# Chunked attention and a bilinear FFN on one core: reordering the first two attention units, and placing the third one step earlier

## The chip, the cores and the metric

The kernel runs on one core of a Trainium2 chip. The metric is the device time of one execution in microseconds (us); lower is better. A run counts as slow when it takes over 1.5% more than the fastest run of its kernel. In the profile lines PE is TensorE, PEld its weight loads, ACT ScalarE, DVE VectorE, POOL GpSimd, SPq the queue of transfers; the granted clock is the share of TensorE's full clock that the profile records. The profile's "span" is shorter than the device time by about 1.8 us, so spans are compared with spans and times with times.

## The reference, cut to what matters

```python
def _attn_ref(q, k, v):                 # B = H = 8, S = 576, D = 64
    q_c = q.reshape(B, H, nc, chunk, D) # chunks of 64 rows attend only to themselves
    scores = scale * np.matmul(q_c, k_c.transpose(0, 1, 2, 4, 3))
    attn = np.exp(scores - np.max(scores, axis=-1, keepdims=True))
    attn = attn / (np.sum(attn, axis=-1, keepdims=True) + 1e-09)
    return np.matmul(attn, v_c).reshape(B, H, S, D)

def _moe_ref(x, w_a, w_b, w_out):       # x: 4608 x 512, d_ff = 1536
    return (x @ w_a) * (x @ w_b) @ w_out
```

The attention output, transposed to tokens x 512, is the `x` of the second function.

## The kernel before: the parts that matter

The 4608 tokens are 18 *units* of 256 for attention and 9 *blocks* of 512 for the FFN. In the traces TensorE's matmuls come in the order in which the program is written (in the timeline below: scores at 13.59, block 0 at 19.65, transposes at 36.14 us), so the schedule is the order of calls. For one unit:

- `cast`: GpSimd (VectorE for q and k of unit 0) turns the loaded float32 q, k and v into bf16 (`q_raw`, `k_raw`, `v_raw`). The weight slices are cast there too, in one queue.
- `transpose_pe`: TensorE transposes q and k; VectorE and ScalarE copy the result to `qkt`.
- `scores`: 32 small matmuls into PSUM, then exp on ScalarE into `E`.
- `sums`: four matmuls with ones, then on ScalarE `ln` and `rs = exp(-ln)`, the inverse of the row sums.
- `values`: 32 small matmuls `E` x v, then VectorE multiplies by `rs` into `xT`, the FFN's input.

`ab_step(K, ft)` is one of the twelve FFN steps of block K, counted from 0: eight matmuls of 512 columns (`wb` and `wa`, four each), a ScalarE copy and a VectorE multiplication. Block 0 needs units 0 and 1. Block 1 begins with the half of it that is unit 2.

```python
        scores(0)                 # prologue, before block 0
        transpose_pe(1)
        sums(0)                   # units 0 to 2: ln, rs, ln, rs, by halves
        scores(1)
        values(0)
        sums(1)
        values(1)
        load(2, "qk")             # after five of the six weight slice pairs
        load_ab(5)
        load(2, "v")
        ...                       # (cut) casts in the same order
        for ft in range(NFT):     # block 0, NFT = 12
            ab_step(0, ft)
            if ft == 7:
                transpose_pe(2)
            if ft == 8:
                slot(2)           # scores(2)
            if ft == 10:
                slot(None, 2)     # sums(2), values(2)
```

The softmax here doesn't subtract the row's maximum and nothing guards it: scores larger than these inputs give would overflow.

## Time and profile before

| What | Value | Where it is read |
|---|---|---|
| time | 330.01 us median of the first three runs (329.94 to 330.35); the profiled run took 330.88 us | list of runs |
| span of the profiled run | 329.1 us | head of the page |
| first block-0 matmul | 19.65 us | timeline |
| k of unit 2 cast | 33.08 to 34.12 us | timeline |
| first block-1 matmul | 45.99 us, after 1.11 us idle | timeline |
| span left after that | 329.1 - 45.99 = 283.1 us | worked out |

The page's chain that ended last, kernel before (share of the span by engine):

```profile
PE 93%; ACT 3%; DMA 1%; DVE 1%; issue 0%; SPq 0%
```

TensorE is the limit. The waits of TensorE in the kernel before (who waited for whom: us in total, times, longest):

```profile
PE ps L156 <- DVE q_raw L144: 5.4, 1, 5.4
PE ps L278 <- DVE xT L239: 3.8, 2, 2.7
PE ps L186 <- ACT qkt L164: 1.6, 2, 1.4
...
```

The first line is the wait for the first q at the start, which the change leaves alone. The second is the two waits that the change is aimed at: 2.7 us before block 0 and 1.1 us before block 1, both for `xT`. The third, and others like it in the prologue, are waits for copies and exp. After 60 us no wait is longer than 0.2 us. Lines of the timeline of the kernel before, picked from all engines (start us, us, engine, line, operation, tiles, and in brackets the idle time before it and what ended it):

```profile
13.59 0.64 PE L186 MATMUL ps<-qkt 64*64 64x64 bf16 x32 [1.23 <-DVE qkt L164]
14.20 0.63 ACT L216 ACTIVATE rs<-ln 128x512 f32<-128x512 f32 x1
14.73 1.07 ACT L194 ACTIVATE E<-ps 128x512 bf16<-128x512 f32 x2
16.47 0.60 ACT L212 ACTIVATE ln<-ps 128x512 f32<-128x512 f32 x1 [0.67 <-PE ps L201]
19.65 1.87 PE L278 MATMUL ps<-xT,wb_162 128*128 128x512 bf16 x4 [2.74 <-DVE xT L239]
33.08 1.04 POOL L144 CAST k_raw<-k_in 128x1024 bf16<-128x1024 f32 x1 [0.97 <-DMA k_in<-in_k_dram]
36.14 0.61 PE L156 MATMUL ps<-identity,k_raw 128*128 128x128 bf16 x8
45.99 0.60 PE L278 MATMUL ps<-xT,wb_162 128*128 128x256 bf16 x4 [1.11 <-DVE xT L239]
```

Two things are to be seen. The scores of unit 1 are done at 14.23 us (13.59 + 0.64), but their exp starts at 14.73 us, as ScalarE ends the inverses of unit 0 (14.83 us; the records overlap a little). The Trainium skill, "TensorE: Matmul & The Clock Gate", Part 1 (Architectural detail), calls ScalarE's queue strict FIFO; this agrees. And k of unit 2 arrives late: its cast ends at 34.12 us, two microseconds before its transposes at 36.14 us.

The four matmuls from 19.65 us take 1.66 us (the next four start at 21.31 us), where four take 0.86 us later on. The same page says in Part 1 that the array starts at half clock. The trace agrees, with 0.43 against 0.216 us for a matmul.

### The profile page before, as it was taken

The page shows a single profiled execution, that of the slowest core. Times are in us where ns is not written, and L with a number is a line of the kernel's source. Part 1 is how long each engine was busy: PE and PEld are TensorE (multiplying, and loading weights), DVE is VectorE, ACT ScalarE, POOL GpSimd, SP SyncE. Part 2 cuts the span into 40 slices and gives each one's busy share as a digit, 9 for nine tenths or more (in the row PEclk, how much of TensorE's full clock was granted, in tenths as well). Part 3 has the DMA queues.
Part 4 walks back from the last instruction along what each step waited for, and adds up shares of the span by engine and source line. Part 5 has one row for each costly group of instructions (what it writes and reads, how often), then busy time and mean ns, then how long its engine had stood idle before and what let it go on. Part 6 is the DMA issues. An engine that isn't in the chain of part 4 may idle for free.

```text
span 329.1 us, 6671 instructions
## 1 busy us (share of the span) xinstructions
PE 311.4 (95%) x2712; PEld 157.4 (48%) x2712; DVE 133.9 (41%) x209; ACT 126.7 (38%) x224; POOL 73.7 (22%) x76
## 2 busy tenths in 40 slices
PE   2669989999999999999999999999999999999994
PEld 1424558776444444444444444444444444444441
DVE  3423454554443434343434343444344434433331
ACT  1633567257352525252525252525252524212200
POOL 1575556632222232132232211200000000000000
PEclk9999999999999999999999999999999999999999
DMA  8999899998979998999988918911120112012114
GB/s 241 320 383 293 225 371 257 276 214 197 173 198 248 228 224 192 225 210 253 203 207 211 231 34 147 241 31 34 42 54 3 34 34 64 1 32 63 35 32 96
DMA packets 139166, 53.91 MB, mean 164 GB/s; under 512 B 114560, under 2 KB 132992, under 8 KB 139136
## 3 DMA queue, kind: packets, MB, share of 16 engines
q1 hardware_dynamic: 139136, 53.49, 68.2%
q8 instruction: 21, 0.34, 0.4%
q14 instruction: 9, 0.07, 0.1%
HBM read 37.75 MB, written 9.44 MB: 143 GB/s over the span
## 4 chain that ended last, share of the span: by engine, by line
PE 93%; ACT 3%; DMA 1%; DVE 1%; issue 0%; SPq 0%
PE ps L278 57%; PE ps L294 28%; PE ps L201 2%; PE ps L156 2%; PE ps L186 2%; PE ps L230 1%; DMA k_in<-in_k_dram 1%; ACT rs L216 1%; ACT ln L212 1%; ACT qkt L164 1%; DVE xT L239 0%; DVE k_raw L144 0%; DVE o_sb L302 0%; ACT E L194 0%; SPq L129 0%
## 5 line engine op out<-in xcount | busy, mean ns | idle before, releaser
L286 ACT CAST b_sb<-ps 128x512 bf16<-128x512 f32 (+1 forms) x120 | 64.4, 546 | 142.6 <-PE ps L278 141.4
L287 DVE TENSOR_TENSOR ab_sb<-ps,b_sb 128x512 bf16<-128x512 f32 (+1 forms) x120 | 75.6, 637 | 94.1 <-PE ps L278 89.7
L294 PEld LDWEIGHTS <-ab_sb 128*128 128x128 bf16 x432 | 42.3, 98 | 50.1
L302 DVE COPY o_sb<-ps 128x512 f32<-128x512 f32 x36 | 24.9, 692 | 56.8 <-PE ps L294 56.8
L239 DVE TENSOR_TENSOR xT<-ps,rs 128x512 bf16<-128x512 f32 x36 | 23.4, 687 | 32.3 <-ACT rs L218 27.6
L144 POOL CAST q_raw<-q_in 128x1024 bf16<-128x1024 f32 x17 | 17.7, 1042 | 60.3 <-DMA q_in<-in_q_dram 52.0
L212 ACT ACTIVATE ln<-ps 128x512 f32<-128x512 f32 x36 | 19.9, 596 | 26.4 <-PE ps L201 26.4
L144 POOL CAST k_raw<-k_in 128x1024 bf16<-128x1024 f32 x17 | 17.7, 1042 | 47.9 <-DMA k_in<-in_k_dram 47.7
L278 PE MATMUL ps<-xT,wb_162 128*128 128x512 bf16 (+1 forms) x80 | 20.2, 378 | 3.8 <-DVE xT L239 3.8
L144 POOL CAST v_raw<-v_in 128x1024 bf16<-128x1024 f32 x18 | 18.8, 1042 | 17.7 <-DMA v_in<-in_v_dram 13.3
L294 PE MATMUL ps<-wo_437,ab_sb 128*128 128x512 bf16 x72 | 21.4, 379 | 0.0
L294 PE MATMUL ps<-wo_443,ab_sb 128*128 128x512 bf16 x72 | 21.4, 379 | 0.0
L294 PE MATMUL ps<-wo_433,ab_sb 128*128 128x512 bf16 x72 | 21.4, 379 | 0.0
L294 PE MATMUL ps<-wo_439,ab_sb 128*128 128x512 bf16 x72 | 21.4, 379 | 0.0
L294 PE MATMUL ps<-wo_441,ab_sb 128*128 128x512 bf16 x72 | 21.4, 379 | 0.0
L294 PE MATMUL ps<-wo_435,ab_sb 128*128 128x512 bf16 x72 | 21.4, 379 | 0.0
L194 ACT ACTIVATE E<-ps 128x512 bf16<-128x512 f32 x36 | 19.3, 587 | 1.8 <-PE ps L186 1.8
L278 PE MATMUL ps<-xT,wa_164 128*128 128x512 bf16 (+1 forms) x80 | 19.7, 370 | 0.0
L278 PE MATMUL ps<-xT,wb_186 128*128 128x512 bf16 (+1 forms) x80 | 18.9, 359 | 0.0
L278 PE MATMUL ps<-xT,wb_170 128*128 128x512 bf16 (+1 forms) x80 | 18.9, 359 | 0.0
L278 PE MATMUL ps<-xT,wb_182 128*128 128x512 bf16 (+1 forms) x80 | 18.8, 358 | 0.0
L278 PE MATMUL ps<-xT,wb_409 128*128 128x512 bf16 (+1 forms) x80 | 18.8, 358 | 0.0
(60 smaller groups left out, 324.5 us busy)
## 6 DMA issues: line engine op xcount, KB each, us to landing
out_dram<-o_sb SPq DMA_DIRECT2D x72, 128.0 KB, 2.4
v_in<-in_v_dram SPq DMA_DIRECT2D x32, 256.0 KB, 4.2
q_in<-in_q_dram SPq DMA_DIRECT2D x23, 256.0 KB, 3.9
k_in<-in_k_dram SPq DMA_DIRECT2D x23, 256.0 KB, 3.7
wst<-in_moe_w_b_dram SPq DMA_DIRECT2D x6, 512.0 KB, 7.3
wst<-in_moe_w_a_dram SPq DMA_DIRECT2D x6, 512.0 KB, 8.0
wst<-in_moe_w_out_dram SPq DMA_DIRECT2D x6, 512.0 KB, 7.2
q_in<-in_q_dram SPq DMA_DIRECT2D x4, 512.0 KB, 5.3
```

Source lines behind the costliest of these rows:

```text
L144: eng.tensor_copy(out=raw[n, U], in_=staged.pop((n, U)))
L156: nc.tensor.transpose(tp[:, i, m, :], src[:, i, 2 * m:2 * m + 2, :].rearrange("p j d -> p (j d)"), identity,)
L186: nc.tensor.matmul(sc[j][cl * 64:cl * 64 + 64, m, g, :], t[j * 64:j * 64 + 64, 1, g, m, cl * 64:cl * 64 + 64], t[j * 64:j * 64 + 64, 0, g, ...
L194: nc.scalar.activation(out=E_of[U][:, j], in_=sc[j], func=AF.Exp, scale=scale)
L201: nc.tensor.matmul(sm[cl][j * 64:j * 64 + 64, :], ones[cl * 64:cl * 64 + 64, :], E[cl * 64:cl * 64 + 64, j].rearrange("p m g s -> p (m g s)"),
L212: nc.scalar.activation(out=ln[:, cl].rearrange("p m n -> p (m n)"), in_=sm[cl], func=AF.Ln)
L239: nc.vector.tensor_tensor(out=x_tiles[K][:, :, c0:c0 + 128], in0=av[cl].rearrange("p m g s -> p m (g s)"), in1=rs[:, cl], op=MULT,)
L278: nc.tensor.matmul(ps[n], w_ab[n, i][:, kt, o:o + 128], xT[:, kt, c0:c1], start=(kt == 0), stop=(kt == NKT - 1),)
L286: nc.scalar.copy(out=b_sb[:, :c1 - c0], in_=ps["wb"])
L287: nc.vector.tensor_tensor(out=ab_tiles[K][:, ft, c0:c1], in0=ps["wa"], in1=b_sb[:, :c1 - c0], op=MULT)
L294: nc.tensor.matmul(o_ps, ab_tiles[K][:, ft, tg * 128:tg * 128 + 128], w_out[ft], start=(ft == 0), stop=(ft == NFT - 1),)
L302: nc.vector.tensor_copy(out=o_sb, in_=o_ps)
```

## The change

Its intent is to shorten both idle stretches. In the prologue, q of unit 1 is transposed before the scores of unit 0, in time in which TensorE waits, and ScalarE computes exp of unit 1 before the inverses of unit 0, which are now one instruction. In block 0, all three parts of unit 2's attention come one step earlier (transposes after step 6, scores after 7, sums and values after 9), and its inverse is one instruction as well.

```diff
-    def transpose_pe(U):
+    def transpose_pe(U, names="qk"):      # q and k can be transposed in two calls
...
-    def sums(U):
+    def sums(U, halves=False):            # None: leaves the inverse to the caller
...
+    def inverse(U, cl=None):              # rs = exp(-ln): one half, or both at once
...
+        transpose_pe(1, "q")
         scores(0)
-        transpose_pe(1)
-        sums(0)
+        transpose_pe(1, "k")
+        sums(0, halves=None)
         scores(1)
+        inverse(0)
         values(0)
-        sums(1)
+        sums(1, halves=True)
         values(1)
...
             ab_step(0, ft)
+            if ft == 6:
+                transpose_pe(2)
             if ft == 7:
-                transpose_pe(2)
-            if ft == 8:
                 slot(2)
-            if ft == 10:
+            if ft == 9:
                 slot(None, 2)
```

More of the change, by code (lines that the diff above doesn't have):

```diff
@@ L147 @@
     qkt = {}
-    def transpose_pe(U):
-        qkt[U] = qkt_pool.tile([128, 2, 2, NKT, 128], BF16, name="qkt")
-        for w, n in ((0, "q"), (1, "k")):
+    def transpose_pe(U, names="qk"):
+        if U not in qkt:
+            qkt[U] = qkt_pool.tile([128, 2, 2, NKT, 128], BF16, name="qkt")
+        for n in names:
+            w = "qk".index(n)
             src = raw.pop((n, U))
@@ L175 @@
     E_of = {}
+    ln_of = {}
     rs_of = {}
@@ L207, in sums @@
                 )
-        ln = sm_pool.tile([128, 2, NKT, 128], FP32, name="ln")
+        ln_of[U] = sm_pool.tile([128, 2, NKT, 128], FP32, name="ln")
         rs_of[U] = sm_pool.tile([128, 2, NKT, 128], FP32, name="rs")
@@ L212, in sums @@
             nc.scalar.activation(
-                out=ln[:, cl].rearrange("p m n -> p (m n)"), in_=sm[cl], func=AF.Ln
+                out=ln_of[U][:, cl].rearrange("p m n -> p (m n)"), in_=sm[cl], func=AF.Ln
             )
-            if U < 3:
-                nc.scalar.activation(out=rs_of[U][:, cl], in_=ln[:, cl], func=AF.Exp, scale=-1.0)
-        if U >= 3:
-            nc.scalar.activation(out=rs_of[U], in_=ln, func=AF.Exp, scale=-1.0)
+            if halves:
+                inverse(U, cl)
+        if halves is False:
+            inverse(U)
+    def inverse(U, cl=None):
+        for c in [slice(0, 2)] if cl is None else [cl]:
+            nc.scalar.activation(
+                out=rs_of[U][:, c], in_=ln_of[U][:, c], func=AF.Exp, scale=-1.0
+            )
     def values(U):
```

## The prediction

> **What bounds the kernel now.** TensorE. The chain of waits puts 93% of the 329.1 us span on it, and the table of waits shows no TensorE wait above 0.2 us after 60 us. So the change can only win what TensorE waits for before block 1, whose first matmul starts at 45.99 us. The timeline shows there: (a) 0 to 19.65 us, the prologue, ending in 2.7 us idle for xT of unit 1; (b) 19.65 to about 24.2 us, 512-column matmuls 0.43 us apart, 0.216 us afterwards. The Trainium skill, "TensorE: Matmul & The Clock Gate", Part 1, says that the array starts at half clock until about 3.4 us of sustained work in a free-running window; this trace agrees (4.6 us slow), though the page's clock row shows full clock; (c) 1.11 us idle at 45.99 us for xT of unit 2.
>
> **Prologue, costed.** q of unit 1 is cast at 8.74 us, so its transposes run while TensorE now idles (7.9 to 9.3 us). Their issue (0.83 us) pushes the scores of unit 0 back about 0.3 us. Both k copies on VectorE then start at about 11.25 instead of 12.25 us, scores of unit 1 at about 12.6 instead of 13.59. Moving exp of unit 1 (1.09 us) ahead of the inverse (1.06 us, measured on the 128x1024 form) keeps it early: sums of unit 1 at about 14.45 instead of 15.85 us, then 0.3 us lost behind the inverse. Last xT near 17.8, first block-0 matmul near 18.5 instead of 19.65: 1.1 us earlier, of which between half and all survives the slow clock, which may be released at the same moment as before.
>
> **Why that is mostly lost.** Attention of unit 2 needs k_raw(2), whose cast on GpSimd ends at 34.12 us behind a DMA wait; casts and loads there wait only for DMA and each other (DMA share 1.11 in this stretch), so they do not move. With transposes after step 6, TensorE would be there at about 33.3 to 33.8 us. I expect a new wait of 0.3 to 0.9 us of the k transposes for k_raw(2), and they start near 34.16 whatever the prologue won. Today's equivalent is 36.14 less one step (1.73), 34.41: net 0.25 us.
>
> **Why the second part pays.** Two steps (3.46 us) then cover the chain ln, ln, inverse, two xT. With one 1.06 us inverse that chain needs about 4.0 us from the sums; values and two steps give 4.1 us. The 1.11 us idle falls to about 0.1. From 34.16: transposes 0.44, five steps 8.65, scores 0.38, sums and values 0.64, waits 0.1: block 1 starts at about 44.4 instead of 45.99 us. v_raw(2) (39.89) and wa of step 10 (38.08) are just in time.
>
> **After.** The later inputs have slack (transposed k of unit 6 lands near 77 us for scores at 80), so about 1.6 us is carried to the end. Matmul count is unchanged.
>
> **Predicted: 328.4 us**, 80% range 327.7 to 329.4. Faster by over 2%: 0.01; within 2%: 0.98; slower: 0.01.
>
> **What would show it.** First block-0 matmul at 18.3 to 18.8 us; a new TensorE (or weight load) wait for k_raw(2), the cast still ending near 34.1 us; idle before block 1 below 0.4 us; start of block 1 at 44.2 to 44.8; then a constant shift of all stages.
>
> **What would make it wrong.** The clock is released a whole window (3.4 us) earlier or later; TensorE then waits longer, or not at all, for k_raw(2), but block 1 hardly moves unless release is late. The loads of unit 2 arrive at another time. The single inverse keeps xT of unit 2 late (up to 0.5 us). A later transposed load turns out to have no slack, so that part of the gain returns as a wait.

## The result, and the profile after

Six runs of each kernel: before 330.22 us median (329.94 to 331.31), after 329.30 us median (329.01 to 329.49). The ratio is 0.9963, with a 95% interval of 0.9946 to 0.9981. Ratios here are the mean time of one kernel's fast runs over that of the other's in the same rounds, so they are not quite the ratio of the medians quoted. The span of the profiled run fell from 329.1 to 327.5 us.

TensorE's waits in the changed kernel (same columns as above; L287 was L278, L158 was L156):

```profile
PE ps L287 <- DVE xT L248: 2.9, 1, 2.9
...
PE ps L158 <- POOL k_raw L144: 0.6, 1, 0.6
...
```

The wait for `xT` now occurs once; the one before block 1 is gone. A wait for `k_raw` has appeared. The same lines of the changed kernel's timeline:

```profile
12.87 0.64 PE L189 MATMUL ps<-qkt 64*64 64x64 bf16 x32 [0.62 <-DVE qkt L166]
13.55 1.09 ACT L197 ACTIVATE E<-ps 128x512 bf16<-128x512 f32 x2 [0.23 <-PE ps L189]
14.52 1.06 ACT L225 ACTIVATE rs<-ln 128x1024 f32<-128x1024 f32 x1
15.46 0.60 ACT L214 ACTIVATE ln<-ps 128x512 f32<-128x512 f32 x1
18.65 1.86 PE L287 MATMUL ps<-xT,wb_162 128*128 128x512 bf16 x4 [2.90 <-DVE xT L248]
32.86 1.04 POOL L144 CAST k_raw<-k_in 128x1024 bf16<-128x1024 f32 x1 [1.12 <-DMA k_in<-in_k_dram]
33.96 0.62 PE L158 MATMUL ps<-identity,k_raw 128*128 128x128 bf16 x8 [0.56 <-POOL k_raw L144]
44.28 0.60 PE L287 MATMUL ps<-xT,wb_162 128*128 128x256 bf16 x4
```

Exp of unit 1 starts at 13.55 instead of 14.73 us, and block 0 at 18.65 instead of 19.65 us. The transposes of k of unit 2 start 0.06 us after the end of its cast (32.86 + 1.04 = 33.90 us). Block 1 starts at 44.28 instead of 45.99 us, 1.71 us earlier, without idle time. From there the span takes 327.5 - 44.28 = 283.2 us, against 283.1 us before (282.9 us in a second profile of it, f4). The small loss is in one place: the scores of unit 6 start 0.53 us after their slot's sums (0.24 us before), and the wait is seen on the weight loads (window 76 to 80 us):

```profile
PEld L189 <- DMA qkt<-k_raw: 0.4, 1, 0.4
```

### The profile page after: what moved, and what is told of

Read it like the earlier page. It is cut to its first block, busy times and chain, and to the rows that moved or that the text cites. A ratio compares the mean times of both kernels' runs of the same rounds, so it can differ in the third digit from the quotient of the medians.

```text
span 327.5 us, 6667 instructions
## 1 busy us (share of the span) xinstructions
PE 311.7 (95%) x2712; PEld 157.3 (48%) x2712; DVE 133.8 (41%) x209; ACT 126.0 (38%) x222; POOL 73.5 (22%) x76
## 4 chain that ended last, share of the span: by engine, by line
PE 80%; DMA 7%; SPq 7%; DVE 1%; ACT 1%; POOL 1%; issue 1%; POOLq 0%; DVEq 0%
PE ps L287 49%; PE ps L303 26%; SPq L117 4%; DMA q_in<-in_q_dram 3%; SPq L129 3%; DMA v_in<-in_v_dram 3%; PE ps L189 1%; DMA qkt<-k_raw 1%; PE ps L239 1%; PE ps L204 1%; DVE qkt L166 1%; ACT rs L225 1%; POOL v_raw L144 1%; POOL q_raw L144 1%; PE ps L158 1%
## 5 line engine op out<-in xcount | busy, mean ns | idle before, releaser
L144 POOL CAST k_raw<-k_in 128x1024 bf16<-128x1024 f32 x17 | 17.7, 1040 | 44.7 <-DMA k_in<-in_k_dram 42.5
L144 POOL CAST v_raw<-v_in 128x1024 bf16<-128x1024 f32 x18 | 18.7, 1040 | 18.9 <-DMA v_in<-in_v_dram 16.2
L287 PE MATMUL ps<-xT,wb_162 128*128 128x512 bf16 (+1 forms) x80 | 20.1, 375 | 2.9 <-DVE xT L248 2.9
L287 PE MATMUL ps<-xT,wa_164 128*128 128x512 bf16 (+1 forms) x80 | 19.7, 370 | 0.0
L225 ACT ACTIVATE rs<-ln 128x1024 f32<-128x1024 f32 (+1 forms) x19 | 19.2, 1012 | 0.6
L287 PE MATMUL ps<-xT,wb_186 128*128 128x512 bf16 (+1 forms) x80 | 18.9, 359 | 0.0
L287 PE MATMUL ps<-xT,wb_170 128*128 128x512 bf16 (+1 forms) x80 | 18.9, 359 | 0.0
L287 PE MATMUL ps<-xT,wb_182 128*128 128x512 bf16 (+1 forms) x80 | 18.8, 358 | 0.0
```

The lines of the kernel that those rows point to most:

```text
L144: eng.tensor_copy(out=raw[n, U], in_=staged.pop((n, U)))
L225: nc.scalar.activation(out=rs_of[U][:, c], in_=ln_of[U][:, c], func=AF.Exp, scale=-1.0)
L287: nc.tensor.matmul(ps[n], w_ab[n, i][:, kt, o:o + 128], xT[:, kt, c0:c1], start=(kt == 0), stop=(kt == NKT - 1),)
```

## The experiments

Theory A: each part of the change would save about a microsecond, but both together are stopped by the arrival of unit 2's k, so they do not add up; later, the transposed load of unit 6 is the next such stop. Rivals: the parts add up (B); the prologue's gain is lost to the slow clock (C); the loads are no limit and the clock is (F, G, H in the texts below). Every run gave a correct result. The first two runs and g1, g2 cut the change into parts, the others move or remove one suspected limit.

### f1: the prologue alone

The changed kernel, with the places of unit 2 set back.

```diff
-            if ft == 6:
+            if ft == 7:
                 transpose_pe(2)
-            if ft == 7:
+            if ft == 8:
                 slot(2)
-            if ft == 9:
+            if ft == 10:
                 slot(None, 2)      # in slot: sums(f, halves=f == 2), two half inverses
```

> The new order of the prologue alone; attention of unit 2 stays at step 7 with its two half inverses. Theory A (the change's two parts overlap: each is bounded by the load of k of unit 2): first block-0 matmul at about 18.65 us, as with both; the k transposes of unit 2 come only at about 35 us, after its cast (34 us), so no wait for k_raw; the 1.1 us idle before block 1 stays; block 1 starts about 1.0 to 1.2 us before that of the kernel before (44.8 to 45.0 us); time -0.9 to -1.2 us. Rival B (parts add up): this part alone is worth the total, 1.6 us in the profiles, less the 1.1 us idle, so about 0.5 us. Rival C (the prologue gain is lost to the slow clock): block 1 moves by less than 0.6 us.

Measured: 330.05 us median (329.35 to 330.61) against 331.02 us of before in the same rounds, ratio 0.9976 (0.9961 to 0.9991). TensorE timeline of f1:

```profile
18.35 1.86 PE L287 MATMUL ps<-xT,wb 128*128 128x512 bf16 x4 [3.29 <-DVE xT L248]
34.72 0.62 PE L158 MATMUL ps<-identity,k_raw 128*128 128x128 bf16 x8
44.58 0.60 PE L287 MATMUL ps<-xT,wb 128*128 128x256 bf16 x4 [1.10 <-DVE xT L248]
```

The first block-0 matmul was 0.3 us earlier than expected (this run had an early clock release in the prologue, see i1). The cast of k ended at 34.66 us, so its transposes were held up by 0.1 us at most (they start 0.54 us after those of q at 34.18 us, where 0.45 us is usual), and the 1.1 us idle stayed. Block 1 started 1.4 us earlier than before. About 0.5 us of that is this run's clock (0.3 us at the start of block 0, and 5.47 instead of 5.68 us from its first step to its third); the 0.9 us left are still more than the 0.6 us that rival C allows, so in the trace it falls.

### f2: the steps alone

The changed kernel with the old prologue (calls joined on one line):

```diff
-        transpose_pe(1, "q"); scores(0); transpose_pe(1, "k"); sums(0, halves=None)
-        scores(1); inverse(0); values(0); sums(1, halves=True); values(1)
+        scores(0); transpose_pe(1); sums(0, halves=True)
+        scores(1); values(0); sums(1, halves=True); values(1)
```

> Attention of unit 2 one step earlier with one inverse, prologue as before. Theory A: first block-0 matmul at 19.65 us; the k transposes reach their place at about 34.4 us, just after the cast of k_raw(2) (34.1 us), so no or little wait (below 0.3 us); idle before block 1 falls from 1.1 to below 0.2 us; block 1 starts at about 44.5 to 44.8 us; time -1.1 to -1.4 us. With f1 the two sum to 2.0 to 2.6 us, more than both together give (1.6 us): the difference, 0.5 to 0.8 us, is the wait for k_raw(2) that only both together show. Rival B (additive): f1 and f2 sum to what both give, and no wait for k_raw(2) differs.

Measured: 329.90 us median (329.33 to 330.19), ratio 0.9966 (0.9952 to 0.9979). TensorE timeline of f2:

```profile
19.63 1.87 PE L287 MATMUL ps<-xT,wb 128*128 128x512 bf16 x4 [2.74 <-DVE xT L248]
34.92 0.61 PE L158 MATMUL ps<-identity,k_raw 128*128 128x128 bf16 x8
45.23 0.60 PE L287 MATMUL ps<-xT,wb 128*128 128x256 bf16 x4
```

There is no wait for k and no idle time before block 1. Block 1 was later than expected (45.23, not 44.5 to 44.8 us) because the clock came late in this run: the third step began 6.2 us after the first, against 5.7 us before and 5.5 us in the changed kernel. Without that, from the third step to block 1 (the former at 25.33, 25.84 and 24.16 us): before 20.66 us, f2 19.39 us, both parts together 20.12 us. The steps save 1.27 us alone but only 0.54 us with the new prologue. The missing 0.73 us is the wait for `k_raw` of the changed kernel, which shows as 0.7 us on its weight loads.

In the times, f1 and f2 save 0.24% and 0.34%, 0.58% or 1.9 us together; both in one kernel save 0.37%, or 1.2 us. The intervals are too wide for the times alone to decide this; the traces decide it.

### g1 and g2: the two halves of the prologue

Both have the old places for unit 2, so that k of unit 2 does not interfere. g1 keeps only the earlier transposes of q, g2 only the earlier exp (each against f1):

```diff
 # g1
-        sums(0, halves=None); scores(1); inverse(0); values(0)
+        sums(0, halves=True); scores(1); values(0)
 # g2
-        transpose_pe(1, "q"); scores(0); transpose_pe(1, "k")
+        scores(0); transpose_pe(1)
```

> Half of the prologue's change: q of unit 1 transposed ahead of the scores of unit 0, but exp of unit 1 still behind both half inverses of unit 0 (attention of unit 2 as before). Theory A (the two halves only pay together, since what one lets go is then held by the other): scores of unit 1 come about 0.7 us earlier (near 12.9 us) but exp of unit 1 starts at about 14.5 us, 0.2 us earlier than before, because the four ln and inverse passes hold ScalarE until then. First block-0 matmul at 19.4 to 19.6 us; time -0.1 to -0.3 us, within noise of the kernel before. Rival D (moving q is what pays): first block-0 matmul near 18.7 us, time -0.8 us.

> The other half: exp of unit 1 ahead of one inverse of unit 0, q of unit 1 transposed where it was. Theory A: scores of unit 1 at 13.6 us as before, exp of unit 1 at about 14.3 us instead of 14.73, and then ln of unit 1 waits for the inverse until about 16.3 us instead of 16.47: first block-0 matmul at 19.4 to 19.6 us; time -0.1 to -0.3 us. g1 and g2 together then give less than half of the 1.0 us that both show in one kernel. Rival E (the order of ScalarE is what pays): near 18.7 us, time -0.8 us.

Measured: g1 330.07 us median, ratio 0.9987 (0.9970 to 1.0005); g2 330.10 us, ratio 0.9988 (0.9970 to 1.0007). The timelines of g1 and then of g2, exp of unit 1, ln of unit 1 and the first block-0 matmul:

```profile
14.53 1.06 ACT L197 ACTIVATE E<-ps 128x512 bf16<-128x512 f32 x2
16.27 0.60 ACT L214 ACTIVATE ln<-ps 128x512 f32<-128x512 f32 x1 [0.67 <-PE ps L204]
19.45 0.58 PE L287 MATMUL ps<-xT,wb 128*128 128x512 bf16 x1 [2.74 <-DVE xT L248]
```

```profile
14.29 1.08 ACT L197 ACTIVATE E<-ps 128x512 bf16<-128x512 f32 x2 [0.76 <-PE ps L189]
15.26 1.06 ACT L225 ACTIVATE rs<-ln 128x1024 f32<-128x1024 f32 x1
16.21 0.60 ACT L214 ACTIVATE ln<-ps 128x512 f32<-128x512 f32 x1
19.39 0.58 PE L287 MATMUL ps<-xT,wb 128*128 128x512 bf16 x1 [2.90 <-DVE xT L248]
```

Each half wins 0.20 to 0.26 us at the start of block 0; together they win 1.00 us. In g1 the scores came at 12.85 us, but exp waited for the four passes of unit 0 until 14.53 us. In g2 exp was early, but ln of unit 1 then waited behind the inverse until 16.21 us. What one half frees, the part that was not changed takes back. Rivals D and E fall. Block 1 did not start earlier than before in either profile (46.22 and 46.12 us).

### f3: one step earlier still

```diff
-            if ft == 6:
+            if ft == 5:
                 transpose_pe(2)
-            if ft == 7:
+            if ft == 6:
                 slot(2)
-            if ft == 9:
+            if ft == 8:
                 slot(None, 2)
```

> The changed kernel with attention of unit 2 one step earlier still (after steps 5, 6 and 8). Theory A: the k transposes would be due at about 31.7 us but wait for the cast of k_raw(2) at 33.9 us: a wait of about 2.2 us instead of 0.6; v_raw(2) (cast ends 40.1 us) is then waited for too, by about 1.6 us less what has been lost already, since its values come one step (1.73 us) earlier; block 1 starts near 46 us, time about 1.3 to 1.8 us over the changed kernel, so about as the kernel before. A rival, that an earlier attention simply helps or does nothing: equal to the changed kernel or faster.

Measured: 331.86 us median (330.62 to 335.57), ratio 1.0050 (1.0006 to 1.0093). The profiled run is the slowest of the six (1.50% above the fastest). Its TensorE timeline:

```profile
34.35 0.62 PE L158 MATMUL ps<-identity,q_raw 128*128 128x128 bf16 x8 [3.76 <-POOL q_raw L144]
36.04 1.04 PE L158 MATMUL ps<-identity,k_raw 128*128 128x128 bf16 x8 [1.07 <-POOL k_raw L144]
36.87 1.91 PE L287 MATMUL ps<-xT,wb 128*128 128x512 bf16 x4
```

The inputs of unit 2 came two microseconds later than in the profile of the changed kernel (k's cast ended at 35.98 instead of 33.90 us), and the wait did more harm than its length: the matmuls after it take 1.71 us for four. The stretches of this run (from:to, length, busy time of each engine, granted clock, DMA share, GB/s):

```profile
34.00:35.00 1.00, 0.62 (x8) 0.45 (x8) 0.00 (x0) 0.00 (x0) 0.35 (x2) 1.00 1.04 340
38.00:40.00 2.00, 2.00 (x6) 0.60 (x4) 0.00 (x0) 1.03 (x2) 1.22 (x2) 0.50 0.52 148
```

The granted clock is 0.50 from about 35 to 42 us. The Trainium skill, "TensorE: Matmul & The Clock Gate", in its table of goals, advises against idle gaps of TensorE over about 3 us between bursts for that reason; here a gap of 3.8 us and another of 1.1 us were followed by it. I had expected the waits and not the clock, so the upper end was far beyond my range; the sign was as expected.

### f4: the kernel before once more

> The kernel before, unchanged, for a second profile and its spread. The profiled run of before took 330.88 us where its median is 330.2, the changed kernel's 329.3 us is its median. Theory A: the runs of before have two levels, near 330.0 and near 331.2 us, and they differ in the moment when the clock is released in block 0 or in a load's arrival (a different start of block 1); a profile near 330.0 shows block 1 start below 45.5 us. Rival: one level with noise; block 1 starts at 46.0 us again, and the difference lies elsewhere in the trace.

Measured: 330.70 us median (330.40 to 331.38), ratio 0.9997; block 1 at 46.21 us, span 329.1 us, nearly the first trace. The profile again fell on a run near 331 us, so this run alone did not settle where the faster level comes from. The clock column of all runs does. The kernel before ran 48 times in the rounds of f, g, h and i, f4 included: the 9 runs whose mean granted clock is recorded as 0.986 or 0.987 took 329.89 to 330.58 us (median 330.03), the 29 runs at 0.999 or 1.000 took 330.86 to 331.56 us (median 331.20), and the other 10 lie on both sides. What the odd figure can mean is seen in i1.

### g3 and g4: the loads of unit 2 first, then also a later place for the scores of unit 6

```diff
 # g3 and g4
-        for i in range(NWP - 1):
+        for i in range(NWP - 2):
             cast_ab(i)
-            if i < 2:
-                load_ab(i + 3)
+            if i == 0:
+                load_ab(3)
+                load(2, "qk")
+            if i == 1:
+                load_ab(4)
...
-        load(2, "qk")
-        load_ab(5)
         load(2, "v")
+        load_ab(5)
         load(3)
         cast(2, "qk")
-        cast_ab(5)
+        cast_ab(4)
         cast(2, "v")
+        cast_ab(5)
         cast(3)
 # g4 alone
-            (23, lambda: slot(6, 5)),
-            (24, lambda: out_step(0, 3)),
+            (23, lambda: slot(None, 5)),
+            (24, lambda: out_step(0, 3)),
+            (24, lambda: scores(6)),
```

> The changed kernel with q and k of unit 2 loaded and cast ahead of the fifth pair of weight slices, and v of unit 2 ahead of the sixth: the wait for k_raw(2) is taken away by an earlier load. Theory A: no TensorE wait for k_raw(2) or v_raw(2); block 1 starts 0.5 to 0.9 us earlier than in the changed kernel (43.4 to 43.8 us for the same moment of clock release). But the scores of unit 6 already wait about 0.3 us for their transposed k there; this wait grows by about what was won, to 0.8 to 1.2 us, so the time is within 0.3 us of the changed kernel (ratio to before 0.995 to 0.998). Rival F (waits of the loads in block 0 cost nothing): block 1 does not move. Rival G (unit 6 is no limit): the time falls by the whole 0.5 to 0.9 us, ratio 0.993 to 0.995.

> As g3, and the scores of unit 6 behind the last output step of block 0 (2.6 us later). Theory A: neither wait is left; time 0.8 to 1.1 us under the changed kernel, ratio to before 0.992 to 0.9945; from the start of block 1 to the end of the span 282.8 to 283.0 us as in the kernel before. Rival G: the same time as g3.

Measured: g3 329.05 us median (328.21 to 330.32), ratio 0.9957 (0.9936 to 0.9978); g4 328.78 us (328.50 to 329.03), ratio 0.9942 (0.9928 to 0.9957). TensorE timeline of g3:

```profile
42.97 0.60 PE L287 MATMUL ps<-xT,wb 128*128 128x256 bf16 x4
77.54 0.45 PE L189 MATMUL ps<-qkt 64*64 64x64 bf16 x32 [0.42 <-DMA qkt<-k_raw]
```

There is no wait for unit 2. Block 1 starts at 42.97 us, 1.31 us before the changed kernel (0.6 us of it is a clock that came early in this run: the third step begins 4.92 us after the first, against 5.51 us), and the wait at unit 6 has grown: these scores follow their sums (76.71 us) by 0.83 us instead of 0.53. In g4 block 1 starts at 43.83 us, although the clock came 0.3 us late there (5.82 us from the first step to the third), and no such wait is left; from there the span takes 326.9 - 43.83 = 283.1 us. Rival F, that the loads cost nothing, falls. The difference of g3 and g4 in time (0.9957 and 0.9942) is within their intervals, so how much the wait at unit 6 costs on average rests on the traces alone; rival G is against the traces and not decided by the times. Both intervals also overlap that of the changed kernel (0.9963, 0.9946 to 0.9981).

### h1 and h2: matmuls that only keep TensorE at work

Six 512-column matmuls of ones whose results nobody reads, in the idle stretch before block 0. h1 is the changed kernel with them, h2 is g4 with them.

```diff
+        keep_busy(6)     # six matmuls warm x warm into a PSUM bank of their own
         for ft in range(NFT):
             ab_step(0, ft)
```

> The changed kernel with six 512-column matmuls of ones, never read, in the 2.9 us in which TensorE waits for xT of unit 1 (cold, they take 2.56 us, so they delay nothing). Theory A: the slow stretch at the start of block 0 (2.8 to 5.6 us long in the traces so far, costing 1.4 to 2.8 us) begins earlier and costs on average 1 to 1.4 us less; but the k transposes of unit 2 still start when the cast of k_raw(2) ends, near 34 us: the wait for unit 2's inputs grows from 0.6 to 1.5 to 2.2 us, block 1 starts at 44.0 to 44.5 us as before, and the time is within 0.4 us of the changed kernel (ratio to before 0.995 to 0.9975). Rival H (k_raw(2) is no fence, the clock is what bounds): block 1 near 43.0 us, time 1.0 to 1.4 us lower (ratio 0.992 to 0.9935).

> The same six matmuls in g4, where unit 2 is loaded early and the scores of unit 6 come late. Theory A: here the saved slow-clock time is kept: block 1 starts at 42.5 to 43.1 us (g4: 43.83), time 0.7 to 1.4 us under g4, ratio to before 0.9895 to 0.992. It may be cut by new waits for v_raw(2) or the sixth weight pair, which then have only some 0.3 us of slack. Rival: no gain, since the array's slow stretch does not count such matmuls.

Measured: h1 331.49 us median (329.11 to 332.56), ratio 1.0009 (0.9973 to 1.0044); h2 327.51 us (326.73 to 328.63), ratio 0.9901 (0.9875 to 0.9926). TensorE timeline of h1 and then of h2:

```profile
18.33 1.02 PE L296 MATMUL ps<-xT,wb 128*128 128x512 bf16 x4 [1.91 <-DVE xT L257]
19.19 1.03 PE L296 MATMUL ps<-xT,wa 128*128 128x512 bf16 x4
32.43 0.62 PE L167 MATMUL ps<-identity,q_raw 128*128 128x128 bf16 x8 [1.86 <-POOL q_raw L153]
34.28 0.62 PE L167 MATMUL ps<-identity,k_raw 128*128 128x128 bf16 x8 [1.23 <-POOL k_raw L153]
44.60 0.60 PE L296 MATMUL ps<-xT,wb 128*128 128x256 bf16 x4
```

```profile
31.37 0.62 PE L167 MATMUL ps<-identity,k_raw 128*128 128x128 bf16 x8 [0.24 <-POOL k_raw L153]
41.69 0.60 PE L296 MATMUL ps<-xT,wb 128*128 128x256 bf16 x4
44.90 0.62 PE L167 MATMUL ps<-identity,k_raw 128*128 128x128 bf16 x8 [1.03 <-POOL k_raw L153]
```

In both, block 0 begins at full clock (0.86 us for four matmuls). In both profiles the clock had already risen in the prologue (scores of unit 1 in 0.45 us, as in i1 below), so the traces show that the six matmuls keep it up, not that they raise it. In h1 this wins nothing: TensorE reaches unit 2 earlier and waits 3.1 us (1.86 + 1.23) for its q and k, and block 1 starts at 44.60 us, no earlier than in the changed kernel (44.28 and 43.85 us in its two profiles). In all three it starts 10.32 us after the transposes of k, and these start when the cast ends (34.22 us in h1). Rival H falls. In h2, where unit 2 is loaded first, block 1 starts at 41.69 us, earlier than I had expected (42.5 to 43.1 us), and the interval of its ratio lies wholly below those of g4 and of the changed kernel. This profile is of the slowest of h2's six runs: it waits 1.6 us for the inputs of unit 3.

Half of my expectation for h1 was wrong: its times are not those of the changed kernel, four of the six are 330.9 us and more. Their mean granted clocks are 0.988 to 0.994. That would fit the slow clock after a long wait of f3, but the fastest run, of 329.11 us, has 0.993 as well, and the profiled run of h1 is one of the two quick ones, so the cause stays open.

### h3: such matmuls in all the prologue's waits

h2 with nine of them before the first q arrives, two before q of unit 1, two before the scores of unit 1, and with the scores of units 7, 9 and so on taken out of their slots to a later place.

```diff
+        keep_busy(9)
         transpose_pe(0)
...
+        keep_busy(2)
         transpose_pe(1, "q")
...
+        keep_busy(2)
         scores(1)
...
-                seq.insert(4, lambda: slot(2 * K + 3, 2 * K + 2))
+                seq.insert(6, lambda: scores(2 * K + 3))
+                seq.insert(4, lambda: slot(None, 2 * K + 2))
```

> h2, with nine more such matmuls while TensorE waits for the first q, two ahead of the transposes of q of unit 1 and two ahead of the scores of unit 1, and with the scores of each odd unit from 7 on set two steps behind its slot, so that its transposed load gains slack. Theory A: if they lift the clock before the prologue's work, its transposes take 0.6 instead of 1.0 us and its matmuls likewise, the first block-0 matmul comes 0.3 to 1.0 us earlier (17.6 to 18.3 us) and block 0 begins at full clock; time 0.2 to 1.0 us under h2. If unit 2's loads or the weights are the next limit, the time stays at h2's and waits for casts show in block 0. The spread between runs shrinks below 0.5 us if the clock is its cause.

Measured: 328.50 us median (327.53 to 328.80), ratio 0.9926 (0.9905 to 0.9947), by the medians slower than h2 by about a microsecond, though the intervals overlap. The prologue went as expected: block 0 starts at 18.02 us and the transposes of q of unit 1 take 0.62 instead of 1.03 us. But TensorE then waits longer for k of unit 2 than in h2, and block 1 starts at 41.84 us, no earlier than there (41.69 us):

```profile
31.52 0.62 PE L167 MATMUL ps<-identity,k_raw 128*128 128x128 bf16 x8 [0.81 <-POOL k_raw L153]
```

From there the span takes 325.9 - 41.84 = 284.1 us, not 283.1. No TensorE wait above 0.2 us appears in the table for this part. Between the sums at 105.65 and those two slots later at 138.98 us there are 33.33 us, where g4 has 33.17 (107.48 to 140.65 us): taking the scores out of their slots costs 0.16 us a block, and over the six blocks (sums at 75.57 to sums at 272.30 us, in g4 77.57 to 273.33 us) 196.73 instead of 195.76 us. So my first edit won nothing by block 1, where unit 2 was the limit again, and my second cost about 1 us. The spread, 1.3 us, did not shrink below 0.5 us either.

### i1: the changed kernel once more

> The changed kernel, unchanged, in five rounds and with a second profile, since its first ratio (0.9963, from three rounds) has a wide interval and its two parts alone gave 0.9976 and 0.9966. Theory A: ratio between 0.994 and 0.9965, so a gain of 1.2 to 2.0 us, less than the 1.9 us that the parts sum to or at most equal to it; the k transposes of unit 2 start within 0.1 us of the end of the cast of k_raw(2), wherever that falls, and from block 1 to the end the span is 282.8 to 283.5 us. If the loads of unit 2 come late in some runs, as in f3, single runs may be up to 1 us longer. Rival B (parts add up): a gain of 1.9 us or more and no wait for k_raw(2).

Measured: 329.95 us median (328.63 to 330.34) against 331.14 us of before, ratio 0.9966 (0.9948 to 0.9983), so the first result is confirmed. TensorE timeline of i1:

```profile
18.40 1.86 PE L287 MATMUL ps<-xT,wb 128*128 128x512 bf16 x4 [3.31 <-DVE xT L248]
33.53 0.62 PE L158 MATMUL ps<-identity,k_raw 128*128 128x128 bf16 x8 [0.41 <-POOL k_raw L144]
43.85 0.60 PE L287 MATMUL ps<-xT,wb 128*128 128x256 bf16 x4
```

The cast of k ended at 33.47 us this time, and the transposes followed at once again. The start of block 1 moved with it: 10.32 us after the k transposes in both profiles of this kernel. This run's mean granted clock is 0.989. Its stretches (columns as in f3):

```profile
13.00:15.00 2.00, 1.48 (x100) 1.10 (x88) 0.00 (x0) 1.96 (x4) 1.51 (x2) 1.00 1.08 375
17.00:19.00 2.00, 0.60 (x2) 0.26 (x2) 0.94 (x2) 0.62 (x1) 1.17 (x2) 0.50 1.08 375
23.00:25.00 2.00, 2.00 (x11) 0.93 (x10) 0.69 (x1) 0.65 (x2) 1.35 (x3) 1.00 1.09 385
```

The clock had been released within the prologue (the scores of unit 1 take 0.45 us here, 0.64 us in the first profile), fell to half at about 15.7 us when TensorE ran dry, and came back near 22.5 us (worked out from the rows of 15 to 17 us, 0.68, and of 22 to 23 us, 0.74). The first profile shows 1.00 over its own slow stretch, and i1 shows 1.00 over its slow transposes at 8.78 us (1.03 us for eight), before the first drop. I infer that the row knows the clock only from the first recorded change on. So in i1 a low figure, 0.989, goes with a *faster* prologue: it counts only the 6.8 us after the drop (f1, at 0.988, is alike). That the quick runs of before (0.986 or 0.987) are of this kind is not shown: none of them was profiled, block 0 of i1 starts only 0.25 us earlier than in the first profile, far less than the 1.2 us between the levels, and in f3 the same figure, 0.987, comes from a late slow stretch. In the changed kernel the figure does not mark quick runs: its four runs at 0.987 to 0.989 took 328.63, 329.01, 329.49 and 330.11 us, spread over nearly its whole range.

## Why the prediction was right or wrong, point by point

The direction, the range and nearly all places in the trace were right.

- **Prologue.** Predicted first block-0 matmul near 18.5 us, measured 18.65 (18.40 in i1). g1 and g2 show that the two edits win this only together, as the prediction's chain of estimates implies.
- **"Why that is mostly lost."** Predicted: a new wait of 0.3 to 0.9 us for `k_raw` of unit 2, with the cast still near 34.1 us. Measured: 0.56 us (0.41 in i1), cast at 33.90 us (33.47). That the cast came within 0.2 us of the forecast is partly luck: in f4, the same kernel as before, it ended at 35.12 us. f1 and f2 show the loss as a failure to add up, 0.73 us; g3 and g4 take the wait away by an earlier load; h1 shows that even a full-speed block 0 wins nothing while the wait is there.
- **"Why the second part pays."** Predicted idle before block 1 about 0.1 us and block 1 at 44.4 us. Measured 0 and 44.28 us.
- **"After."** Predicted: the later inputs have slack. This was wrong by 0.3 us in the first profile: the scores of unit 6 waited for their transposed k. In i1 they did not. The slack had been read from one trace, at 3 us.
- **"Predicted: 328.4 us."** This was 0.9 us too low, though in the range. The step that failed is the subtraction: I took 1.6 us, read from the trace of a 330.88 us run, from the median of three runs, 330.01 us. From the run that was traced it gives 329.3 us, which is the median measured. Over all rounds the gain is 0.34 to 0.37%, 1.1 to 1.2 us, not 1.6: the kernel before takes about 1.2 us less (330.03 against 331.20 us) in the runs whose mean clock is recorded as 0.986 or 0.987, and the three runs I started from lie at that level by their times while the traced one does not. I had seen the two clocks but not asked whether the trace was of a typical run. Why the changed kernel does not gain as much from such runs was not traced; that it then waits longer for unit 2 is a likely reason, not a shown one.

What stays open: why the loads of unit 2 end 2 us apart from run to run (cast of k from 33.47 to 35.98 us in kernels with the same order of loads), what the quick runs of before gain their 1.2 us by, and what h1's slow runs lose their time to.

The best version run is h2: the change, with unit 2's loads moved ahead, the scores of unit 6 later and six idle matmuls, at 327.51 us, 0.99% under the kernel before. h3 without its second edit, which might be a microsecond faster than h3 was, was not run.

## What to carry to other kernels

When an edit lets the limiting engine reach a place earlier, look up when the inputs of that place arrive: the gain ends there, and two edits that win a microsecond each can share one limit. Two edits on one chain of dependences can also be worth little alone and much together, so a part that tests flat is not thereby useless. Take a predicted difference from the time of the run that was traced, and ask first whether that run is a typical one.

## What the Trainium skill lacked or had wrong

- "TensorE: Matmul & The Clock Gate", Part 1: it names about 3.4 us of sustained work, in a free-running window. Here the slow stretch of block 0 lasted about 4.5 us in the kernel before (11 matmuls, from 19.65 to 24.2 us) and about 2.8 us in f3 (18.7 to 21.5 us), and there was none when TensorE had been kept at work just before (h1). It puts the fall of the clock after idle gaps of about 3 us (table of goals): in i1 the clock rose within a prologue of small matmuls and fell about 0.6 us after the last of them, and this run, the fastest of its six (328.63 us), shows a *lower* mean granted clock (0.989).
- The same page, Part 4, says that the full clock does not engage for transposes. In these traces eight 128x128 transposes take 1.03 us at the slow clock and 0.61 us after the clock has risen, so they can run at it; whether transposes alone would raise it, no run shows.
- No page names this fault of a profile's clock row: it can show 1.00 over a slow stretch at the start, until the first change is recorded: kernel before, 0.43 us for a 512-column matmul at a row of 1.00.
- No page gives a figure for setting a group of small matmuls apart among large ones ("TensorEngine Tiling (Array Packing)" says only that a change of tiling mode drains the engine): it cost 0.16 us a block in h3, with no wait recorded.
